# A gated mix of a long convolution and a windowed attention: GpSimd's arithmetic moved to VectorE, the large loads moved to GpSimd's queue

## The chip, the cores and the metric

The kernel runs on one core of one Trainium2 chip. The metric is the device time of one execution in microseconds (us). A core has TensorE (PE in the profile, with its weight loads as PEld), VectorE (DVE), ScalarE (ACT), GpSimd (POOL) and SyncE (SP). Each works through its own instruction stream in order. Transfers are issued by SP, ACT or POOL from that same stream and run on the core's 16 DMA engines.

## The reference

Two branches share the input `x = A_q` (2048 rows of 640) and are mixed row by row by a gate `g`. Branch A is a 4-tap convolution of `k` along the sequence, times `v`, then a long convolution with `ssm_k` (by FFT), plus `kv * ssm_D`, times `q`. Branch B is an attention of 32 heads of width 20, in which each query sees 8 keys, two rows apart.

```python
g = sigmoid((x * gate_w).sum(-1, keepdims=True))
# branch A
k_shift = sum over t of k_pad[:, t:t+S, :] * shift_k[:, 3-t]
kv = k_shift * v
y = irfft(rfft(kv padded to 2S) * rfft(ssm_k padded to 2S))[:S] + kv * ssm_D
a = q * y
# branch B
q, k, v = split(x @ wqkv)
logits = q . k[pos - 2*w] * Dh**-0.5 for w in 0..7, masked where pos - 2*w < 0
b = (softmax(logits) . v[pos - 2*w]) @ wo
return g * a + (1 - g) * b
```

## The kernel before

All work of the core is cut into small units (one PSUM slot each, four slots of two banks), and every kind of unit is a Python generator. A planner (`Plan.run`) merges the generators into one order per engine: it keeps a model of each engine's and queue's time, and at every step takes the request with the smallest start time plus 120 ns times a priority (`PRI`). It also chooses ACT or DVE for each copy out of PSUM (`AD` requests). What the planner decides is an order only. On the chip each engine runs its list in order and waits on semaphores.

The stages, with the names that the profile shows:

- **Head.** Eight loads of `x` (`xn`) are transposed (L440, 10 matmuls each) into `xT`, copied by DVE. From `xT` come 18 value projections (`psv`, L510, 10 matmuls of 320 columns each, copied to `VW`) and 30 query and key projections (`pj`, L557, 10 matmuls each, cast to `stg`). One gate projection (`gps`, L524) gives `g_nat` and `omg = 1 - g`.
- **Fragments.** `fragger` (L596) moves each finished `stg` by SBUF-to-SBUF transfers on SP into the key and query sets `kb`, `qb` (three of each), whose mask rows GpSimd has written before (L420 to L422).
- **Attention.** For each of 8 groups of 4 heads: scores `sc` (L618), exponentials on ACT (L625, 10 per group, into `ETall`), weighted sums `O` (L646), normalisation on DVE (L655, L658) into `oS`.
- **Short convolution.** `k` is loaded into `kin` (part of tile `KX`) and `v` into `vin`, eight loads each. DVE makes 4 multiplications and 3 additions for each chunk of 8 of the 64 row positions (`taps`, L454 and L461), and the product with `v` (L465). GpSimd does the same for row positions 0 to 7 (`conv_g`, buffer `pgb`).
- **Transforms.** Eight loads bring `ssm_k` to `h_lin` (in the space of `xn`), GpSimd adds `ssm_D` (L726). Then for the two halves P of the channels, and for both `h` and the convolved product `u`: first stage (L679, 10 units of 8 matmuls), second stage (L695, 11 units of 8 or 12). `h` of half 0 lands in tile `SX` (the space of `KX`, so it waits for the end of the convolution), of half 1 in `Hs`, `u` in `UC`. Swapped copies `Hw` of `h` come by transfers. Products on DVE (L779, 16 in all, 8 for each half). Inverse first stage (L791, 10 units of 16 matmuls for each half), cast into `UC`.
- **Output projection.** `oS` is transposed (L809) to `oT`, 16 units `op` (L825) are scaled by `omg` on ACT into `bl`.
- **End.** `load_q` (L841) loads `q` once more, 4 transfers, into the space of `SX`, after the inverse of half 0 has read it. `qscale` (L848) multiplies it by `g`, 16 instructions of 128x640. `final` (L869) makes the last inverse stage, six groups of three row blocks (the sixth has one): ACT casts it to `yb`, DVE multiplies by the scaled `q` (L881) and adds `bl` (L883), SP stores (L886).

In this kernel SP issues every large load, in one stream with the fragments: a request of `load` waits in the planner until the transfers before it are nearly done (`bg=1500`). ACT issues 16 transfers before its first computation (L403 to L411). GpSimd writes masks and ones, issues five small transfers, computes its share of the convolution, adds `ssm_D` and scales `q`. Each queue uses eight completion semaphores in turn, so a transfer waits for the one eight places ahead of it.

Of the kernel before, what the change touches and what calls it, by code (L numbers as in the profile page):

```python
# [13 lines left out]
ALU = mybir.AluOpType  # L14
# [32 lines left out]
CR = 8  # L47
GR = 8
# [81 lines left out]
class Req:  # L130


    def __init__(self, engs, cost=0.0, deps=(), take=0, give=(), n=0, move=0.0, pri=None, mode=None, bg=None, mm=0, lean=0.0):
        self.engs, self.cost, self.deps, self.take, self.give, self.n, self.move = engs, cost, deps, take, give, n, move
        self.pri, self.mode, self.bg, self.mm, self.lean = pri, mode, bg, mm, lean
# [4 lines left out]
LEAN_QK = 1040.0  # L140
LEAN_V = -285.0
LEAN_H = -39.0
PRI = dict(loads=0, fragger=0, xpose=1.5, score_gen=0.0, pv_gen=1.0, conv=3.0, conv_v=5.5, conv_g=0, conv_end=0, qkproj=2.1, vproj=2.7, gate=5.7,
           load_G=0, h_slot=0, u_slot=0, swaps=0, load_T=0, op_tr=-7.6, outproj=14.1, load_q=0, qscale=0, final=3.6, h_stream=(6.3, 5.2),
           u_stream=(10.8, 10.0), mults=(-3.3, 5.2), inverse1=(8.0, 7.7))
# [4 lines left out]
class Plan:  # L150


    def __init__(self, nslots):
        self.at = dict(P=0.0, A=0.0, D=0.0, G=0.0, S=0.0, Q=0.0)
        self.mode = None
        self.count = 0
        self.page = 0.0
        self.pipe = 0.0
# [13 lines left out]
    def start(self, r, e):  # L172
# [12 lines left out]
        if r.bg is not None:  # L185
            t = max(t, self.pipe - r.bg)
# [10 lines left out]
    def run(self):  # L197
        while self.streams:
# [31 lines left out]
            if r.move:  # L230
                at = max(self.pipe, st + 1300.0)
                self.pipe = at + r.move
                g.done = Ev(self.pipe + 700.0, "X")
# [15 lines left out]
def kernel(  # L249
# [96 lines left out]
    def load(name, dst, src, us, deps=(), bg=None, q="S"):  # L346
        g = yield Req(q, 500.0, deps, move=us, bg=bg, pri=None if bg is None else 1)
# [5 lines left out]

    def rows32(ap, q, n0, n1):
        return raw(ap, n0 * D + QC * q, [[64 * D, 32], [D, n1 - n0], [1, QC]])

    def loads():
# [7 lines left out]
        for a in range(4, 8):  # L365
            yield from load_x(a)
        for c in (1, 0):
            for q in range(4):
                yield from load(f"k{q}{c}", kin[32 * q:32 * q + 32, 3 + 32 * c:35 + 32 * c, :], rows32(k2, q, 32 * c, 32 * c + 32), 1400.0, (), 1500.0)
        for c in range(2):  # L370
            for q in range(4):
                yield from load(f"v{q}{c}", vin[32 * q:32 * q + 32, c], raw(v2, QC * q + 80 * c, [[64 * D, 32], [D, 64], [1, 80]]), 2050.0, (), 1500.0)
        yield Req("S", 1.0, [ev("convG")])
        h_lin = p0.tile([128, 80, 2, 64], BF, name="h_lin", tag="HL")
        st["h_lin"] = h_lin
        for c in range(2):
            for q in range(4):
                yield from load(f"h{q}{c}", h_lin[32 * q:32 * q + 32, :, c, :],
                                raw(A_ssm_k, (160 * q + 80 * c) * S, [[64, 32], [S, 80], [1, 64]]), 2200.0, (), 1500.0)

    def load_G():
        yield Req("S", 1.0, [ev("conv"), ev("grow"), ev("vproj")])
# [18 lines left out]

    def heads():
# [3 lines left out]
        for q in range(4):  # L406
            nc.scalar.dma_start(wraw[32 * q:32 * q + 32].rearrange("p c j -> p (c j)"), raw(A_shift_k, 4 * QC * q, [[0, 32], [1, 4 * QC]]))
        for q in range(4):
            for a, b in ((1, 17), (17, 32)):
                nc.scalar.dma_start(kin[32 * q + a:32 * q + b, 0:3, :], raw(k2, (64 * a - 3) * D + QC * q, [[64 * D, b - a], [D, 3], [1, QC]]))  # L410
        nc.scalar.dma_start(F[:], cf["F"].ap())  # L411
# [515 lines left out]
```

## Time and profile before

| | |
|---|---|
| median of 3 runs | 300.77 us (298.35 to 301.0) |
| the profiled execution, its own time | 300.68 us |
| its span, first to last instruction | 298.9 us |
| PE busy | 222.3 us (74%) |
| DVE busy | 208.6 us (70%) |
| ACT busy | 153.8 us (51%) |
| POOL busy | 77.9 us (26%) |
| granted TensorE clock, mean | 0.833 |

Busy shares are means over stages with different limits, so the profile is read by stage. Stretches are cut at events of PE: first score matmul at 57.3 us, end of the last query or key projection at 134.2, end of the last weighted sum at 161.5, last second-stage transform matmul at 215.7, first inverse matmul at 231.2, end of the inverse at 249.3. What ends last in each stretch sets its length.

### The profile page before, as it was taken

To read this page: it belongs to the slowest core of one execution; us is meant where nothing else is said; L and a number is where in the kernel's file an instruction comes from. 1 tells how busy PE (TensorE), PEld (TensorE's weight loads), DVE (VectorE), ACT (ScalarE), POOL (GpSimd) and SP (SyncE) were. 2 spreads that over 40 slices of the span, in tenths; PEclk is the share of its full clock that TensorE was granted. 3 is DMA by queue.
4 is the path that set the end of the run, shared out by engine and by line. 5 is a ranking of instruction groups with operands and counts; after the bars stand their busy time and mean duration, and the time that the engine had idled before them with its cause. 6 is when DMAs were issued, how large, how long until landed. Compare 5 with 4: busy or idle time off the path is not lost. (4 is left out here: it accounts for less than half of the span.)

```text
span 298.9 us, 8211 instructions
## 1 busy us (share of the span) xinstructions
PE 222.3 (74%) x3639; PEld 171.5 (57%) x3646; DVE 208.6 (70%) x214; ACT 153.8 (51%) x186; POOL 77.9 (26%) x57
## 2 busy tenths in 40 slices
PE   3789996379898999598889998975899997122000
PEld 2779784146655666366667887764577996111000
DVE  1135899999769999497888899858499343035472
ACT  0232210244454875288988699876465876023210
POOL 3996099810100000100000000000000000199990
PEclk9999997778977999796555999999599999655555
DMA  7999982918955999445800003999400009702333
GB/s 245 311 266 165 153 117 52 140 22 132 133 86 108 133 135 120 83 110 156 270 8 5 3 2 68 219 219 212 133 0 2 2 15 210 133 3 68 92 106 89
DMA packets 58587, 33.82 MB, mean 113 GB/s; under 512 B 48184, under 2 KB 55096, under 8 KB 57912
## 3 DMA queue, kind: packets, MB, share of 16 engines
q1 hardware_dynamic: 57000, 32.50, 56.5%
q10 hardware_dynamic: 1392, 0.80, 1.0%
q8 instruction: 28, 0.46, 0.7%
q14 instruction: 7, 0.06, 0.1%
q0 software_dynamic: 160, 0.00, 0.1%
HBM read 20.01 MB, written 2.62 MB: 76 GB/s over the span
## 5 line engine op out<-in xcount | busy, mean ns | idle before, releaser
L625 ACT ACTIVATE ETall<-sc 121x912 bf16<-121x912 f32 (+1 forms) x80 | 64.1, 854 | 38.2 <-PE sc L618 36.5
L848 POOL TENSOR_SCALAR SX<-SX,g_nat 128x640 bf16<-128x640 bf16 x16 | 30.8, 1939 | 138.5 <-DMA SX<-in_A_q_dram 138.5
L557 PE MATMUL pj<-xT,Wqk 128*128 128x342 bf16 (+1 forms) x300 | 56.8, 343 | 4.1 <-DVE stg L278 3.6
L557 PEld LDWEIGHTS <-Wqk 128*128 128x128 bf16 x300 | 30.0, 105 | 22.4 <-issue 4.5
L618 PE MATMUL sc<-qb,kb 31*128 31x114 bf16 x576 | 24.1, 246 | 14.1 <-DMA vin<-in_A_v_dram 4.9
L278 DVE CAST stg<-pj 128x684 bf16<-128x684 f32 (+1 forms) x30 | 26.6, 888 | 9.0 <-PE pj L557 4.5
L510 PE MATMUL psv<-KX,xT 128*121 128x320 bf16 x180 | 30.4, 323 | 2.9 <-ACT VW L276 1.9
L454 DVE TENSOR_TENSOR KX<-KX 128x1280 bf16<-128x1280 bf16 x28 | 30.9, 1116 | 2.1 <-DMA g_nat<-KX 1.8
L510 PEld LDWEIGHTS <-xT 128*121 128x121 bf16 x180 | 25.9, 148 | 5.3 <-issue 3.5
L618 PEld LDWEIGHTS <-kb 31*128 31x128 bf16 x576 | 14.6, 107 | 25.1 <-issue 19.6
L276 ACT CAST VW<-psv 121x640 bf16<-121x640 f32 x17 | 11.6, 697 | 31.1 <-PE psv L510 31.1
L881 DVE TENSOR_TENSOR SX<-yb,SX 128x1920 bf16<-128x1920 bf16 (+1 forms) x6 | 9.2, 1538 | 25.4 <-POOL SX L848 25.4
L276 ACT CAST UC<-s 128x960 bf16<-128x960 f32 (+2 forms) x25 | 22.4, 966 | 8.2 <-PE s L695 8.0
L695 PEld LDWEIGHTS <-SX 64*128 64x128 bf16 x512 | 20.0, 98 | 10.7 <-issue 9.6
L825 PE MATMUL op<-wo,oT 128*128 128x512 bf16 (+1 forms) x153 | 24.5, 312 | 0.4
L461 DVE TENSOR_TENSOR KX<-KX 128x1280 bf16<-128x1280 bf16 x21 | 23.4, 1114 | 1.3 <-DMA g_nat<-KX 0.9
L876 ACT CAST yb<-i 128x960 bf16<-128x960 f32 (+1 forms) x12 | 9.9, 873 | 25.4 <-DVE SX L881 17.8
L278 DVE CAST UC<-s 128x1024 bf16<-128x1024 f32 (+1 forms) x17 | 19.3, 1193 | 4.1 <-PE s L695 3.3
L869 PE MATMUL i<-UC,T 32*32 32x160 bf16 x512 | 6.9, 288 | 19.6 <-ACT yb L876 9.8
L825 PEld LDWEIGHTS <-oT 128*128 128x128 bf16 x160 | 16.8, 148 | 7.0 <-issue 1.5
L278 DVE COPY xT<-tx 128x1280 bf16<-128x1280 bf16 x8 | 6.5, 822 | 20.0 <-PE tx L440 20.0
L278 DVE CAST SX<-s 128x1024 bf16<-128x1024 f32 (+1 forms) x15 | 17.1, 1187 | 1.7 <-PE s L679 1.6
(65 smaller groups left out, 373.6 us busy)
## 6 DMA issues: line engine op xcount, KB each, us to landing
xn<-in_A_q_dram SPq DMA_DIRECT2D x8, 320.0 KB
KX<-in_A_k_dram SPq DMA_DIRECT2D x8, 320.0 KB
vin<-in_A_v_dram SPq DMA_DIRECT2D x8, 320.0 KB
h_lin<-in_A_ssm_k_dram SPq DMA_DIRECT2D x8, 320.0 KB
Hw<-SX SPq DMA_DIRECT2D x4, 640.0 KB
Hw<-Hs SPq DMA_DIRECT2D x4, 640.0 KB
SX<-in_A_q_dram SPq DMA_DIRECT2D x4, 640.0 KB
out_dram<-SX SPq DMA_DIRECT2D x20, 120.0 KB
```

What stands on the lines that cost most here:

```text
L276: nc.scalar.copy(dst, src)
L278: nc.vector.tensor_copy(dst, src)
L454: eng.tensor_tensor(d, kin[:, n + 3 - j:n + 3 - j + m, :], w.to_broadcast([128, m, QC]), ALU.mult)
L461: eng.tensor_tensor(ta if j else dst, ta, tb, ALU.add)
L510: nc.tensor.matmul(ps[0:BK, n0 // 320, 0:320], lhsT=xT[:, dt, s0:s0 + BK], rhs=Wv[:, dt, n0:n1], start=(dt == 0), stop=(dt == NDT - 1))
L557: nc.tensor.matmul(ps[:, i, 0:n], lhsT=Wqk[:, dt, w, 128 * ft:128 * ft + 128], rhs=xT[:, dt, s0:s0 + n], start=(dt == 0), stop=(dt == NDT ...
L618: nc.tensor.matmul(sc[:, hh, BQ * bb:BQ * bb + BQ], lhsT=kb[r:r + DH + NF, BK * b:BK * b + 128], rhs=qb[r:r + DH + NF, BQ * b:BQ * b + BQ] ...
L625: nc.scalar.activation(ETall[0:BK, e, :, 0:BQ * nb], sc[0:BK, :, 0:BQ * nb], ACT.Exp, scale=SCALE)
L695: nc.tensor.matmul(ps[:, c, 160 * jj:160 * jj + 160], lhsT=st["G"][rows, j0 + jj, rr, :], rhs=Am[rows, rr].rearrange("p o (q j) l -> p j ( ...
L825: nc.tensor.matmul(op[:, n0:n1], lhsT=oT[:, ft].rearrange("p h m a -> p a (h m)")[:, t, :], rhs=wo[:, ft, n0:n1], start=(ft == 0), stop=(f ...
L848: nc.gpsimd.tensor_scalar(qg[:, t, :], qg[:, t, :], g_nat[:, t:t + 1], None, ALU.mult)
L876: nc.scalar.copy(yb[:, 0:m, 320 * k:320 * k + 320].rearrange("p n (q c) -> p q n c", q=2), pss[k][:, :, 0:160 * m].rearrange("p q (n c) -> ...
```

## The change

GpSimd keeps its mask and constant writes and the one addition of `ssm_D`. Its share of the convolution (`conv_g`) and the scaling of `q` go to DVE. The convolution now runs over all 64 row positions in chunks of 11 (five of 11 and one of 9: 42 instructions of up to 1760 elements where there were 49 of 1280), the product with `v` in 4 pieces of 32 positions. The loads of `k`, `v`, `ssm_k`, `G`, `wo`, `T` and `q` are issued by GpSimd, in a generator `bulk` of their own, as are 13 of the 16 transfers that ACT issued (4 of `wraw`, 8 of the rows before `kin`, and `F`). `masks(2)` and the ones in `ETall` and `VW` are written between the loads of `k` and `v`. DVE clears a buffer and PE runs 8 matmuls of 512 columns on it before the first transpose. The planner's leans and priorities are other numbers, its model has a transfer pipe for each queue, and `bg` is gone.

```diff
-CR = 8
-GR = 8
+CR = 11
+WARM = 8
...
-LEAN_QK = 1040.0
-LEAN_V = -285.0
-LEAN_H = -39.0
...
+LEAN_QK = -370.0
+LEAN_V = 53.0
+LEAN_H = 195.0
...
+    def bulk():
         for c in (1, 0):
             for q in range(4):
-                yield from load(f"k{q}{c}", kin[32 * q:32 * q + 32, 3 + 32 * c:35 + 32 * c, :], rows32(k2, q, 32 * c, 32 * c + 32), 1400.0, (), 1500.0)
+                yield from load(f"k{q}{c}", kin[32 * q:32 * q + 32, 3 + 32 * c:35 + 32 * c, :],
+                                raw(k2, 32 * c * D + QC * q, [[64 * D, 32], [D, 32], [1, QC]]), 2200.0, [ev("x3")], "G")
+        g = yield Req("G", 4000.0)
+        masks(2)
...
+        nc.gpsimd.memset(ETall[:, :, :, 3 * BQ:], 1.0)
...
-        for q in range(4):
-            nc.scalar.dma_start(wraw[32 * q:32 * q + 32].rearrange("p c j -> p (c j)"), raw(A_shift_k, 4 * QC * q, [[0, 32], [1, 4 * QC]]))
...
+        z = pab[:, 0].rearrange("p n c -> p (n c)")
+        nc.vector.memset(z, 0.0)
+        wu = psp.tile([128, 2, 512], F32, name="wu", tag="ps0")
+        for n in range(WARM):
+            nc.tensor.matmul(wu[:, n % 2, :], lhsT=z[:, 0:128], rhs=z[:, 0:512], start=True, stop=True, skip_group_check=True)
...
-        for n in range(64 - CR, GR - 1, -CR):
...
+        hi = 64
+        while hi:
+            m = min(CR, hi)
+            n = hi - m
...
-    def conv_g():
...
-            for n in range(GR, 64, 28):
...
+            for n in range(0, 64, 32):
...
     def load_q():
-        yield Req("S", 1.0, [ev("i10")])
+        yield Req("G", 1.0, [ev("i10")])
...
-            nc.sync.dma_start(qg[32 * g:32 * g + 32], raw(x2, (32 * (g // 2) + g % 2) * D, [[64 * D, 32], [2 * D, 16], [1, D]]))
+            nc.gpsimd.dma_start(qg[32 * g:32 * g + 32], raw(x2, (32 * (g // 2) + g % 2) * D, [[64 * D, 32], [2 * D, 16], [1, D]]))
...
     def qscale():
         for t in range(16):
-            r = yield Req("G", 700.0, [ev("qg"), ev("gate")])
+            r = yield Req("D", 310.0, [ev("qg"), ev("gate")])
             qg = st["qg"]
-            nc.gpsimd.tensor_scalar(qg[:, t, :], qg[:, t, :], g_nat[:, t:t + 1], None, ALU.mult)
+            nc.vector.tensor_scalar(qg[:, t, :], qg[:, t, :], g_nat[:, t:t + 1], None, ALU.mult)
```

GpSimd's stream from its second mask set on, before (lines of the kernel before):

```order
L420 MEMSET kb_81 128x8
L421 COPY kb_81<-mm 128x2178
L422 COPY qb_82<-mm 128x2052
L423 MEMSET ETall 128x16x128
L424 MEMSET VW 128x576
L426 MEMSET VW 7x32 x2
L427 DMA wgz<-in_gate_w_dram 128x5x1
L429 DMA Dz<-in_A_ssm_D_dram 1x16x10 x4
L454 ISA
L454 TENSOR_TENSOR pgb<-KX 128x1280 x2
```

and in the changed kernel (its own line numbers; L346 is the helper that issues a load, `KX` holds `kin`):

```order
L440 DMA F<-cf_F 128x384
L346 DMA KX<-in_A_k_dram 32x32x160 x8
L410 MEMSET kb_81 128x8
L411 COPY kb_81<-mm 128x2178
L412 COPY qb_82<-mm 128x2052
L372 MEMSET ETall 128x16x128
L373 MEMSET VW 128x576
L375 MEMSET VW 7x32 x2
L346 DMA vin<-in_A_v_dram 32x64x80 x8
L346 DMA h_lin<-in_A_ssm_k_dram 32x80x64 x8
L728 ISA
L728 TENSOR_TENSOR h_lin<-h_lin,Dz 128x160
```

The arithmetic on `pgb` is gone, and 24 loads stand around the third mask set and the ones, with nothing of another kind between the last two blocks.

VectorE's stream at the start of the convolution, before (L278 copies out of PSUM, L454 and L461 are the convolution's multiplications and additions):

```order
L278 COPY xT<-tx 128x2x5x128 x4
L278 CAST stg<-pj 128x2x342
L278 COPY xT<-tx 128x2x5x128 x2
L469 COPY KX<-KX 128x640
L278 COPY xT<-tx 128x2x5x128
L278 CAST stg<-pj 128x2x342
L278 COPY xT<-tx 128x2x5x128
L454 TENSOR_TENSOR KX<-KX 128x1280 x2
L278 CAST stg<-pj 128x2x342
```

and in the changed kernel (L276 copies out of PSUM, L465 and L472 are the convolution; the rows left out are more of L465 and L472 alone):

```order
L419 MEMSET KX 128x880
L276 COPY xT<-tx 128x2x5x128 x8
L480 COPY KX<-KX 128x640
L465 TENSOR_TENSOR KX<-KX 128x1760 x2
L472 TENSOR_TENSOR KX<-KX 128x1760
...
L276 CAST stg<-pj 128x2x363
L465 TENSOR_TENSOR KX<-KX 128x1760
```

21 instructions of the convolution now stand before VectorE's first cast of a projection. Of the 30 such casts VectorE keeps 17 and ScalarE has 13.

VectorE's stream at the end, before (L881 and L883 are the last product and sum) and after it the changed one (L850 is the scaling of `q`, L883 and L885 the last product and sum):

```order
L278 CAST UC<-i_4005 128x128x8
L278 CAST UC<-i_4061 128x128x8
L881 TENSOR_TENSOR SX<-yb_4002,SX 128x1920
L883 TENSOR_TENSOR SX<-SX,bl 128x1920
L881 TENSOR_TENSOR SX<-yb_4002,SX 128x1920
```

```order
L276 CAST UC<-i_3949 128x128x8
L276 CAST UC<-i_4005 128x128x8
L850 TENSOR_SCALAR SX<-SX,g_nat 128x640 x16
L883 TENSOR_TENSOR SX<-yb_4040,SX 128x1920
L885 TENSOR_TENSOR SX<-SX,bl 128x1920
```

The 16 scalings stand between the last cast of the inverse and the first product. On PE the tenth and last inverse unit of half 0, which `load_q` waits for, is the 12th of the 20 inverse units with 3 `op` units among them, where it was the 15th with none.

## Rows read from the trace of the kernel before

**Rows 1.** The chain that ended last, in order of time: start us, us, what.

```profile
231.37 13.41 PE i L791 x240
...
246.19 14.27 DMA SX<-in_A_q_dram
...
272.90 16.75 POOL SX L848 x9
...
289.67 1.76 DVE SX L881
...
293.03 0.02 issue
293.05 0.49 DVE SX L883
```

**Rows 2.** Groups of instructions: busy us and mean ns, idle before, releaser.

```profile
L848 POOL TENSOR_SCALAR SX<-SX,g_nat 128x640 bf16<-128x640 bf16 x16 | 30.8, 1939 | 138.5 <-DMA SX<-in_A_q_dram 138.5
```

**Rows 3.** By stretch: length, busy PE, PEld, DVE, ACT, POOL (instructions); clock, DMA share, GB/s.

```profile
57.30:134.20 76.90, 68.75 (x972) 44.08 (x976) 66.41 (x90) 42.57 (x53) 5.17 (x4) 0.88 0.74 107
134.20:161.50 27.30, 24.16 (x562) 18.43 (x564) 22.53 (x28) 24.25 (x31) 0.00 (x0) 0.56 0.40 124
161.50:215.70 54.20, 45.93 (x857) 38.22 (x858) 44.63 (x40) 40.97 (x47) 0.00 (x0) 0.91 0.53 118
215.70:231.20 15.50, 15.31 (x109) 11.40 (x111) 14.31 (x11) 9.69 (x13) 0.00 (x0) 1.00 0.00 1
```

**Rows 4.** Timeline of DVE: start us, us, engine, line, operation, idle before.

```profile
50.01 3.11 DVE L454 TENSOR_TENSOR KX<-KX 128x1280 bf16<-128x1280 bf16 x1
...
72.12 0.82 DVE L461 TENSOR_TENSOR KX<-KX 128x1280 bf16<-128x1280 bf16 x1
...
291.46 1.16 DVE L883 TENSOR_TENSOR SX<-SX,bl 128x1920 bf16<-128x1920 bf16 x1
```

**Rows 5.** Timeline of POOL, same columns.

```profile
7.97 2.00 POOL L421 COPY kb<-mm 128x2178 bf16<-128x2178 bf16 x1 [4.35 <-DMA mm<-ca_mm]
...
25.07 2.03 POOL L429 DMA_DIRECT2D Dz<-in_A_ssm_D_dram x4
...
49.37 3.07 POOL L461 TENSOR_TENSOR pgb<-pgb 128x1280 bf16<-128x1280 bf16 x1
...
121.25 0.94 POOL L726 TENSOR_TENSOR h_lin<-h_lin,Dz 128x160 bf16<-128x160 bf16 x1 [39.33 <-DMA qb<-stg]
```

**Rows 6.** Timeline of ACT, its first computation.

```profile
13.33 1.28 ACT L276 ACT_TABLE_LOAD   x1 [13.33 <-DMA KX<-in_A_k_dram]
```

**Rows 7.** Timeline of PE in the head.

```profile
6.36 2.89 PE L510 MATMUL psv<-KX,xT 128*121 128x320 bf16 x10 [1.01 <-DMA KX<-in_B_wqkv_dram]
...
23.18 1.52 PE L510 MATMUL psv<-KX,xT 128*121 128x320 bf16 x10
24.54 0.72 PE L440 MATMUL tx<-ident,xn 128*128 128x128 bf16 x10
25.09 1.52 PE L510 MATMUL psv<-KX,xT 128*121 128x320 bf16 x10
...
27.01 1.62 PE L557 MATMUL pj<-xT,Wqk 128*128 128x342 bf16 x10
...
57.30 0.56 PE L618 MATMUL sc<-qb,kb 31*128 31x114 bf16 x8 [4.94 <-DMA vin<-in_A_v_dram]
```

**Rows 8.** Timeline of SP's queue: start of the first issue, time over all.

```profile
15.68 14.99 SPq L348 DMA_DIRECT2D KX<-in_A_k_dram x8
...
47.69 5.30 SPq L596 DMA_DIRECT2D kb<-stg x7
```

**Rows 9.** Groups of DVE instructions, shapes kept apart.

```profile
L881 DVE TENSOR_TENSOR SX<-yb,SX 128x1920 bf16<-128x1920 bf16 x5 | 8.7, 1748 | 25.4 <-POOL SX L848 25.4
...
L469 DVE COPY KX<-KX 128x640 bf16<-128x640 bf16 x1 | 0.5, 483 | 0.0
...
L538 DVE TENSOR_SCALAR omg<-g_nat 128x16 f32<-128x16 f32 x1 | 0.2, 174 | 0.0
```

More of the change, by code (lines that the diff above doesn't have):

```diff
@@ L130, with __init__ @@
 class Req:
[L133 removed]
+    def __init__(self, engs, cost=0.0, deps=(), take=0, give=(), n=0, move=0.0, pri=None, mode=None, mm=0, lean=0.0):
         self.engs, self.cost, self.deps, self.take, self.give, self.n, self.move = engs, cost, deps, take, give, n, move
[L135 removed]
+        self.pri, self.mode, self.mm, self.lean = pri, mode, mm, lean
 LAT = {("P", "A"): 230.0, ("P", "D"): 230.0, ("A", "P"): 120.0, ("D", "P"): 120.0, ("A", "D"): 100.0, ("D", "A"): 100.0}
 SWITCH = 110.0
[L140 to L145 removed]
+LEAN_QK = -370.0
+LEAN_V = 53.0
+LEAN_H = 195.0
+PRI = dict(loads=0, fragger=0, xpose=-8.5, score_gen=-1.4, pv_gen=1.9, conv=3.5, conv_v=5.1, bulk=0, conv_end=0, qkproj=2.0, vproj=-7.0, gate=5.7,
+           load_G=0, h_slot=0, u_slot=0, swaps=0, load_T=0, op_tr=6.4, outproj=4.9, load_q=0, qscale=0, final=11.8, h_stream=(2.5, 4.7),
+           u_stream=(5.8, -3.9), mults=(-7.4, 9.9), inverse1=(2.9, 1.2))
 PAGE = 256
@@ L230, in run @@
             if r.move:
-                at = max(self.pipe, st + 1300.0)
-                self.pipe = at + r.move
-                g.done = Ev(self.pipe + 700.0, "X")
+                at = max(self.pipe[e], st + 1300.0)
+                self.pipe[e] = at + r.move
+                g.done = Ev(self.pipe[e] + 700.0, "X")
                 self.lane[e].append(g.done.t)
@@ L344, with load @@
     st = {}
-    def load(name, dst, src, us, deps=(), bg=None, q="S"):
-        g = yield Req(q, 500.0, deps, move=us, bg=bg, pri=None if bg is None else 1)
+    def load(name, dst, src, us, deps=(), q="S"):
+        g = yield Req(q, 700.0 if q != "G" else 300.0 + 0.7 * us, deps, move=us)
         dict(S=nc.sync, Q=nc.scalar, G=nc.gpsimd)[q].dma_start(dst, src)
@@ L469, in conv @@
         nc.vector.tensor_copy(wl, wraw.rearrange("p c j -> p j c"))
-        at("wl", 0.0)
-        c0 = 60.0 + 0.55 * CR * QC
-        for n in range(64 - CR, GR - 1, -CR):
-            g = yield Req("D", c0, [ev(f"k{q}{c}") for q in range(4) for c in range(2) if c or n < 35])
-            for _ in taps(nc.vector, n, CR, pab[:, 0], pab[:, 1], kin[:, n + 3:n + 3 + CR, :]):
+        hi = 64
+        while hi:
+            m = min(CR, hi)
+            n = hi - m
+            c0 = 150.0 + 0.525 * m * QC
+            g = yield Req("D", c0, [ev(f"k{q}{c}") for q in range(4) for c in range(2) if (c or n < 35) and (hi > 32 or not c)])
+            for _ in taps(nc.vector, n, m, pab[:, 0, 0:m], pab[:, 1, 0:m], kin[:, n + 3:n + 3 + m, :]):
                 g = yield Req("D", c0)
+            hi = n
         mark("convD", g)
@@ L612, in score_gen @@
                 for k in range(2):
-                    g = yield Req("P", 2 * nb * 28.0 + 30.0, [ev(f"set{t}"), ev("ET")], take=1, mode="s", mm=2 * nb)
+                    g = yield Req("P", 2 * nb * 28.0 + 30.0, [ev(f"set{t}")], take=1, mode="s", mm=2 * nb)
                     sc = psum(g, "sc")
@@ L889 @@
     heads()
-    for gen in (loads, fragger, xpose, score_gen, pv_gen, conv, conv_v, conv_g, conv_end, qkproj, vproj, gate, load_G, h_slot,
+    for gen in (loads, fragger, xpose, score_gen, pv_gen, conv, bulk, conv_v, conv_end, qkproj, vproj, gate, load_G, h_slot,
                 u_slot, swaps, load_T, op_tr, outproj, load_q, qscale, final):
```

88 lines of the change are left out of this document (40 added, 48 removed).

## The prediction, made before the changed kernel ran

> **What bounds the kernel now.** I read the chain that ended last first, then the stretches, then single timelines. The chain [rows 1] shows PE at the inverse until 231.37 + 13.41 = 244.8 us, then nothing but the reload of `q` until 246.19 + 14.27 = 260.5, then GpSimd's scaling (one piece alone is 16.75 us), then VectorE's last pair. The scaling is 16 instructions and 30.8 us [rows 2]. VectorE ends at 293.05 + 0.49 = 293.5, and the span at 298.9, so the stores cost 5.4 us more. From the end of the inverse of half 0 (call it X, 244.8) the tail is 298.9 - 244.8 = 54.1 us, in which PE has little to do.
>
> Ahead of X, PE is busy in most of every stretch [rows 3], but not at one limit: from 57.3 to 134.2 PE has 68.75 and VectorE 66.41 of 76.9 us, from 134.2 to 161.5 ScalarE has 24.25 of 27.3 (its exponentials), from 161.5 to 215.7 nobody is over 46 of 54.2 and the copies out of PSUM share the work. In the head PE waits: ScalarE computes nothing before 13.3 us, because it issues transfers [rows 6], and the first score stands behind 4.94 us of waiting for loads in SP's stream [rows 7]. Where GpSimd computes beside VectorE, VectorE's convolution instruction takes 3.11 us, and 0.82 where GpSimd is idle [rows 4, 5].
>
> **The head.** PE's work ahead of the first score is, in the changed order, 8 transposes, 18 value projections, 9 `pj` and the gate, where it was 8, 15 and 8. From start to start a warm value projection takes 24.54 - 23.18 = 1.36 us and a transpose 25.09 - 24.54 = 0.55 [rows 7]. A `pj` shows 1.62, some 0.15 of it under the next unit as with the value projection: 1.5. The gate is put at 1.2, an estimate from its 20 matmuls against a unit's 10 of about two thirds the width. The first value projection started at 6.36 and ran cold (2.89 us against 1.52). Eight matmuls of 512 columns ahead of it take about 0.4 us each cold (2.89 for 10 of 320 columns, scaled), so 3.5 us, start after a clearing of 880 elements, and end near 5.5; the value projections begin at 7 but warm. ScalarE has three transfers left instead of 16, so its copies no longer hold PE. The key set of the first group needs 18 value and 6 `pj` units: 7 + 7 x 0.55 + 18 x 1.36 + 6 x 1.5 = 44.3, its cast 0.9, and then the fragments. Lower bound: seven issues of 5.30 us [rows 8] and 2 for landing, 52.5; upper: as before, 57.3 - 47.7 = 9.6 from the first issue, 54.8. I take 52.5, as no load stands in SP's stream any more. That is 4.8 us earlier, with 3 x 1.36 + 1.5 + 1.2 = 6.8 us more of PE's work done: 11.6 us ahead.
>
> **The convolution and the loads.** GpSimd reaches the loads of `k` so: masks at 8.0 [rows 5], two sets of 3.9, four small clears and transfers (4.0), nine small transfers at 2.03 / 4 = 0.51 each (4.6): 24.5 us. What one issue of 1024 rows costs on its queue no row shows: below, 0.51; above, 14.99 / 8 = 1.87, SP's [rows 8]. I take 1.5, near the upper row, which is of the same transfer. The four loads that the first chunk needs are issued by 30.5 and landed by about 35.5. One instruction of 1760 elements is put between 0.82 for 1280 and 1.16 for 1920 [rows 4], 1.08; 21 of them stand ahead of VectorE's first cast, so that cast comes at 58 us, and PE's tenth `pj` (done near 54) waits for it, with three other slots to go on. Of VectorE's remaining work to the last cast (21 x 1.08, 4 products of about 1.45, 16 casts of 0.88, four normalisations of 2.6) there are 53 us: it could end at 111. PE needs 76.9 - 6.8 = 70.1 us from 52.5, 122.6. So PE's pace decides, and VectorE's block costs nothing unless `k` is late. If nothing of the block hides, it costs 58 - 52.5 = 5.5 us, and this stays in the upper end. GpSimd's own eight instructions like the one shown [rows 5] cost VectorE some 2.3 us each, but before 60 us, so this gain is already in the head.
>
> The 16 loads of `v` and `ssm_k` follow the masks and ones (about 9 us), from 46 us. At 1.5 to 3.0 us each (the same upper row, doubled for rows twice as many) they end between 70 and 94. They are needed near 100 and 125. Before, the last landed at 121.25 [rows 5], so there is room.
>
> **The middle.** From the last `pj` to the last weighted sum both orders hold the same 216 score and 240 sum matmuls, ScalarE bound: 27.3 us again, 122.6 + 27.3 = 149.9. From there to the last second-stage matmul (54.2 before) PE loses three `op` units of 1.41 (11 of them fill the 15.5 us [rows 3]) and 48 second-stage matmuls, done earlier, and gains 16 of the first stage: 5.3 us less, 48.9, to 198.8. VectorE's products move behind this point, but ten `op` units (14.1 us) cover the eight of half 0 (11.3). Then X lies after 12 inverse units of 13.41 / 15 = 0.894 and three `op`: 14.1 + 10.7 + 4.2 = 29.0, as before (29.1). X = 227.8.
>
> **The tail.** The reload takes 15.7 us again, and 0.5 more through GpSimd. Scaling on VectorE: no row has it. Below it, the scalar form on 16 elements, 0.174; above it, a copy of the same 640 elements at 0.483 [rows 9]; between, 0.33, so 16 x 0.33 = 5.3 us (2.8 to 7.7). Then five pairs of 1.75 and 1.16 [rows 4, 9] and one of 0.98: 15.5. The stores 5.4. The sum is 16.2 + 5.3 + 15.5 + 5.4 = 42.4 instead of 54.1. PE's last stage starts 8 inverse and two `op` units after X, 10 us, under the reload.
>
> The Trainium skill, "VectorE: DVE Perf Modes", the perf-mode tier table, gives this kind of instruction four elements a cycle in bf16. By its arithmetic the scaling would be an estimated 0.32 us each, 5.2 in all; no run here shows it yet.
>
> Sum: 227.8 + 42.4 = 270.2 us of span, against 298.9; the time lies 1.8 above the span (300.68, beside a median of 300.77): **272 us**.
>
> **The rivals.**
> *Descriptors held by VectorE.* If GpSimd can't write its transfers while VectorE reads two SBUF operands, as it can't compute beside it (3.11 against 0.82 [rows 4]), the 16 loads advance only in VectorE's gaps. Its 51 us of convolution lie in the 70 from 36 to 106, which leaves 27%: 1.5 / 0.27 = 5.6 us each, 46 + 90 = 136 for the last, needed at 125, PE's first `h` unit being stuck in order. Cost 10 to 13 us: **284**. For it, the contention in the rows; against it, that those rows are of arithmetic that reads.
> The Trainium skill, "SBUF — State Buffer", "Who interferes with whom", has a lock that blocks GpSimd's descriptors under VectorE's two-port copies and scalings, and exempts two-input operations because they take the read side only. By that rule the loads here are free, and only the 16 scalings, behind all loads, would hold anything; the 3.11 us agree with its clause on reads.
>
> *The head's gain is given back.* VectorE and PE hold 89% and 86% of the stretch from 57.3 [rows 3]; if the order's waits stretch with what starts earlier, only the tail is won: 300.7 - 11.7 = **289**. For it, that two engines are near full there; against it, that 13 casts go to ScalarE, which has 42.57 of 76.9.
>
> *Slower: GpSimd's queue can't feed the transforms.* The place is the addition of `ssm_D`, which waits for the last `ssm_k` load; PE's first `h` unit stands behind it. My gain is 28.5 us, so it is lost when `h_lin` is whole later than 125 + 28.5 = 153. From 24.5 that is 128 us for 24 loads, 5.4 each. Before, they spanned 15.68 to 121.25, 4.4 each, but with SP waiting for casts in between; `k` alone took 1.87. At 6 us each: 168, **316**. Nothing shows such a price; no row shows the queue loaded either.
>
> *More.* Granted clock was 0.88 from 57.3; without stalls, 12% of 68.75 is 8 us: **264**.
>
> **How the numbers follow.** The forecast with its bounds (scaling -2.5 to +2.4, fragments +2.3, block +5.5, middle -5 to +5) holds 264 to 280, chance 0.63. More than it, below 264, 0.10. Descriptors held or late `k`, 280 to 287, 0.11; head given back, 287 to 297, 0.08; within 1% of 300.8, 0.03; slower by over 1% (GpSimd's queue), 0.05. One per cent is about what a measurement of this kernel can tell from no change. A range of 260 to 288 leaves out some 0.04 below and 0.14 above. Faster 0.92, same 0.03, slower 0.05.
>
> **What would show it.** Right: first score near 52; VectorE's convolution near 1.08 us each throughout; last `pj` near 123; the addition of `ssm_D` before 120; X near 228; no POOL in the chain's end; scalings near 0.33. Wrong: VectorE's first convolution after 42 us, or PE idle for `h_lin`, points to the queue; a last `pj` after 130 to the head's gain given back; scalings that begin later than 17 us after X to the reload.

## The result, and the profile after

The changed kernel takes **282.56 us** (median of 4 runs, 280.38 to 282.92) against 299.86 for the kernel before: a ratio of 0.941, 95% interval 0.934 to 0.948. The forecast was 272 with a range of 260 to 288. The profiled execution took 282.82 us with a span of 281.0 at a mean granted clock of 0.837.

Parts of the page after: busy time; the span in 40 slices of 7.0 us (PE, VectorE, ScalarE, DMA in tenths); the queues (packets, MB, share of 16 engines); the chain by line.

```profile
PE 216.7 (77%) x3654; PEld 166.9 (59%) x3654; DVE 189.8 (68%) x213; ACT 161.8 (58%) x197; POOL 60.5 (22%) x79
...
PE   6999999216900898999985999888999999991320
...
DVE  2142079940502899999885878999998995411992
ACT  1333543033801387886884878999965588771460
...
DMA  6953999999995114233598100019579000495085
...
q0 software_dynamic: 4368, 14.84, 29.0%
q1 hardware_dynamic: 8072, 18.04, 26.3%
...
PE psv L512 9%; DMA kb<-stg 8%; PE op L827 7%; PE pj L559 6%; DMA g_nat<-KX 5%; DMA SX<-in_A_q_dram 5%; PE s L697 5%; DMA qb<-stg 5%; DVE UC L276 4%; PE sc L620 4%; PE i L793 4%; DVE Hs L276 3%; DVE stg L276 3%; DVE KX L465 3%; PE O L648 3%; DVE SX L885 2%
```

GpSimd's scaling, which stood in the chain before [rows 1, 2], is gone. In its place 18% of the span is DMA of things that are small: fragments of `kb` and `qb`, and `g_nat`. The slices say where: PE reads 2, 1 in the eighth and ninth and 0, 0 in the twelfth and thirteenth, while the DMA engines are at 9 without a break from the fifth to the twelfth slice.

The forecast and the trace, stage by stage (us; X is the end of the inverse of half 0, as in the prediction):

| | first score | last `pj` | last weighted sum | last second stage | X | end of span |
|---|---|---|---|---|---|---|
| forecast | 52.5 | 122.6 | 149.9 | 198.8 | 227.8 | 270.2 |
| after | 61.0 | 137.7 | 170.6 | 212.0 | 241.1 | 281.0 |
| stage after, minus forecast | +8.5 | +6.6 | +5.6 | -7.5 | +0.1 | -2.5 |

The timeline of PE after (start us, us, what, idle time before and its releaser) shows the first two differences.

```profile
36.14 10.44 PE L559 MATMUL pj<-xT,Wqk 128*128 128x342 bf16 x70
46.51 1.26 PE L526 MATMUL gps<-xT,wgz 128*32 128x512 bf16 x20
47.71 3.08 PE L559 MATMUL pj<-xT,Wqk 128*128 128x342 bf16 x20
61.00 0.25 PE L620 MATMUL sc<-qb,kb 31*128 31x114 bf16 x1 [10.22 <-DMA kb<-stg]
...
76.75 0.76 PE L648 MATMUL O<-VW,ETall 121*128 121x21 bf16 x24
92.63 2.73 PE L559 MATMUL pj<-xT,Wqk 128*128 128x342 bf16 x9 [15.12 <-DVE oS L660]
```

All that the forecast put ahead of the first score (18 value projections, 9 `pj`, the gate) is done at 47.71 + 3.08 = 50.8. Then PE stands for 10.2 us, and again for 15.1. What released it, from the chain that ended last (start us, us, what):

```profile
45.55 12.76 DMA qb<-stg
58.32 11.01 DMA kb<-stg
...
74.63 15.13 DMA g_nat<-KX
89.88 1.07 DVE KX L472
...
141.54 9.47 DMA kb<-stg
```

A fragment is at most 85 KB and `g_nat`'s four transfers are 2 KB each; they take 9 to 15 us to land. By stretch (length; busy PE, PEld, DVE, ACT, POOL; clock, DMA share, GB/s), the DMA engines are full through PE's first wait and up to the second, and behind the second PE is busy nearly all the time:

```profile
50.00:61.00 11.00, 0.78 (x6) 0.32 (x4) 9.20 (x9) 1.55 (x3) 2.40 (x3) 0.64 1.05 163
61.00:77.00 16.00, 12.39 (x170) 7.48 (x171) 4.66 (x5) 9.05 (x12) 5.93 (x5) 0.72 1.04 175
77.00:93.00 16.00, 0.88 (x23) 0.67 (x20) 3.08 (x5) 0.73 (x1) 1.28 (x1) 0.60 0.70 93
93.00:138.00 45.00, 43.95 (x735) 28.71 (x735) 43.61 (x59) 33.83 (x43) 2.18 (x4) 0.95 0.30 61
```

VectorE stands in the same place: a convolution instruction, line 472, waits 15.45 us. In the tail its 16 scalings take 4.82 us (5.3 forecast), and a product takes 1.15 where 1.75 was forecast. VectorE's timeline:

```profile
73.52 0.92 DVE L276 CAST stg<-pj 128x726 bf16<-128x726 f32 x1
89.88 1.07 DVE L472 TENSOR_TENSOR KX<-KX 128x1760 bf16<-128x1760 bf16 x1 [15.45 <-DMA g_nat<-KX]
...
258.71 4.82 DVE L850 TENSOR_SCALAR SX<-SX,g_nat 128x640 bf16<-128x640 bf16 x16 [10.97 <-DMA SX<-in_A_q_dram]
263.45 1.15 DVE L883 TENSOR_TENSOR SX<-yb,SX 128x1920 bf16<-128x1920 bf16 x1
```

SP's queue starts these issues early enough, but they stretch (start of the first, time over all):

```profile
41.50 5.46 SPq L598 DMA_DIRECT2D qb<-stg  x7
47.06 11.91 SPq L598 DMA_DIRECT2D kb<-stg  x7
...
68.57 6.56 SPq L535 DMA_DIRECT2D g_nat<-KX  x4
...
76.07 15.29 SPq L598 DMA_DIRECT2D kb<-stg  x7
```

The seven issues of `kb` took 5.30 us before [rows 8] and take 11.91 and 15.29 now, because SP waits for earlier transfers of its own: over the whole run nine times for `qb`, 8.7 us, and twice for `g_nat`, 10.1. So a late landing is paid in the queue as well; in the chain above a landing of `qb` and one of `kb` stand one behind the other. Meanwhile GpSimd's loads of `v` are issued from 39.77 at 1.05 us each, those of `ssm_k` from 48.83 to 73.41 at 1.19 each, and the page has their median time from issue to landing: 13.6 and 17.2 us.

**Theory A**: the loads no longer stand in SP's queue, but they stand on the same 16 DMA engines, up to eight at a time, and SP's fragments and `g_nat` come through late among them. **Rivals**: the wait for `g_nat` alone is the loss (B); it is the number of small rows, not the bytes, that is in the way (A1 against A2); SP's issues or the new order set it (C). And in the tail: that the scaling is not what gave the 18 us.

### The profile page after: what moved, and what is told of

It is laid out like the page before. It is cut to its first block, busy times and chain, and to the rows that moved or that the text cites. A ratio compares the mean times of both kernels' runs of the same rounds, so it can differ in the third digit from the quotient of the medians.

```text
span 281.0 us, 8233 instructions
## 1 busy us (share of the span) xinstructions
PE 216.7 (77%) x3654; PEld 166.9 (59%) x3654; DVE 189.8 (68%) x213; ACT 161.8 (58%) x197; POOL 60.5 (22%) x79
## 2 busy tenths in 40 slices
DMA packets 13034, 33.81 MB, mean 120 GB/s; under 512 B 2764, under 2 KB 6872, under 8 KB 12360
## 4 chain that ended last, share of the span: by engine, by line
PE 43%; DVE 26%; DMA 23%; SPq 3%; issue 2%; POOL 1%; ACT 1%; DVEq 0%
PE psv L512 9%; DMA kb<-stg 8%; PE op L827 7%; PE pj L559 6%; DMA g_nat<-KX 5%; DMA SX<-in_A_q_dram 5%; PE s L697 5%; DMA qb<-stg 5%; DVE UC L276 4%; PE sc L620 4%; PE i L793 4%; DVE Hs L276 3%; DVE stg L276 3%; DVE KX L465 3%; PE O L648 3%; DVE SX L885 2%
## 5 line engine op out<-in xcount | busy, mean ns | idle before, releaser
L559 PE MATMUL pj<-xT,Wqk 128*128 128x342 bf16 (+1 forms) x300 | 51.6, 326 | 15.5 <-DVE oS L660 15.1
L559 PEld LDWEIGHTS <-Wqk 128*128 128x128 bf16 x300 | 28.8, 101 | 32.6 <-issue 16.4
L465 DVE TENSOR_TENSOR KX<-KX 128x1760 bf16<-128x1760 bf16 (+1 forms) x24 | 24.8, 1042 | 11.6 <-DMA KX<-in_A_k_dram 11.2
L274 ACT CAST stg<-pj 128x684 bf16<-128x684 f32 (+1 forms) x13 | 9.5, 744 | 36.9 <-DMA kb<-stg 27.6
L472 DVE TENSOR_TENSOR KX<-KX 128x1760 bf16<-128x1760 bf16 (+1 forms) x18 | 18.8, 1044 | 15.9 <-DMA g_nat<-KX 15.4
L512 PE MATMUL psv<-KX,xT 128*121 128x320 bf16 x180 | 25.7, 299 | 1.4 <-DVE xT L276 1.4
L274 ACT CAST UC<-s 128x1024 bf16<-128x1024 f32 (+1 forms) x24 | 22.6, 1000 | 4.0 <-PE s L697 3.0
L276 DVE CAST stg<-pj 128x726 bf16<-128x726 f32 (+1 forms) x17 | 15.2, 894 | 11.1 <-DMA g_nat<-KX 10.3
L276 DVE CAST UC<-s 128x960 bf16<-128x960 f32 (+2 forms) x18 | 19.9, 1139 | 1.1 <-PE s L697 1.0
L276 DVE CAST SX<-s 128x1024 bf16<-128x1024 f32 (+1 forms) x16 | 18.8, 1195 | 2.5 <-PE s L697 1.9
L827 PEld LDWEIGHTS <-oT 128*128 128x128 bf16 x160 | 16.5, 147 | 5.7
L793 PE MATMUL i<-F,Hw 128*128 128x128 bf16 x160 | 18.3, 219 | 0.0
L831 ACT ACTIVATE bl<-op,omg 128x640 bf16<-128x640 f32 x16 | 12.7, 795 | 9.2 <-PE op L827 9.2
L793 PEld LDWEIGHTS <-Hw 128*128 128x128 bf16 x160 | 17.9, 113 | 0.0
## 6 DMA issues: line engine op xcount, KB each, us to landing
vin<-in_A_v_dram POOLq DMA_DIRECT2D x8, 320.0 KB, 13.6
h_lin<-in_A_ssm_k_dram POOLq DMA_DIRECT2D x8, 320.0 KB, 17.2
SX<-in_A_q_dram POOLq DMA_DIRECT2D x4, 640.0 KB, 10.2
```

The costliest lines, as they stand in the source:

```text
L274: nc.scalar.copy(dst, src)
L276: nc.vector.tensor_copy(dst, src)
L465: eng.tensor_tensor(d, kin[:, n + 3 - j:n + 3 - j + m, :], w.to_broadcast([128, m, QC]), ALU.mult)
L472: eng.tensor_tensor(ta if j else dst, ta, tb, ALU.add)
L512: nc.tensor.matmul(ps[0:BK, n0 // 320, 0:320], lhsT=xT[:, dt, s0:s0 + BK], rhs=Wv[:, dt, n0:n1], start=(dt == 0), stop=(dt == NDT - 1))
L559: nc.tensor.matmul(ps[:, i, 0:n], lhsT=Wqk[:, dt, w, 128 * ft:128 * ft + 128], rhs=xT[:, dt, s0:s0 + n], start=(dt == 0), stop=(dt == NDT ...
```

## The experiments

Times are medians; ratios are to the kernel before as it ran beside each, with 95% intervals, and are not quotients of the medians shown. From each trace, which is of one execution (of e13 the fastest, 294.8; of e5 the slowest, 285.6): the start of the first score and of the last instruction of three groups, the last issue of `q`'s reload, and the end of the span.

| kernel | us | ratio | first score | last `pj` | last sum | last 2nd stage | reload issued | end |
|---|---|---|---|---|---|---|---|---|
| before | 299.9 | 1 | 57.3 | 133.9 | 161.4 | 215.5 | 246.2 | 298.9 |
| after | 282.6 | 0.941 (0.934-0.948) | 61.0 | 137.4 | 170.4 | 211.8 | 243.7 | 281.0 |
| e4: before, scaling on VectorE | 283.5 | 0.943 (0.935-0.951) | 56.9 | 131.7 | 159.0 | 212.8 | 243.5 | 280.2 |
| e13: after, scaling on GpSimd | 298.3 | 0.994 (0.987-1.002) | 60.8 | 136.2 | 168.2 | 209.7 | 241.6 | 293.0 |
| e5: after, no warming | 282.8 | 0.938 (0.933-0.942) | 62.3 | 137.5 | 170.3 | 215.2 | 247.0 | 283.7 |
| e1: after, own `grow` | 278.2 | 0.926 (0.918-0.933) | 61.3 | 132.5 | 165.8 | 207.2 | 239.1 | 276.5 |
| e3: after, long rows | 273.6 | 0.911 (0.903-0.918) | 65.6 | 129.3 | 161.2 | 202.7 | 234.5 | 271.7 |
| e8: after, 4 in flight | 276.9 | 0.920 (0.916-0.924) | 60.5 | 132.0 | 163.7 | 205.1 | 237.0 | 274.2 |
| e2: after, 2 in flight | 267.9 | 0.888 (0.878-0.897) | 54.3 | 123.6 | 156.1 | 197.1 | 229.0 | 266.4 |
| e10: e2, no warming | 269.3 | 0.899 (0.895-0.904) | 55.5 | 122.2 | 154.3 | 198.6 | 230.5 | 267.6 |
| e6: e2 and e1 | 265.0 | 0.881 (0.876-0.885) | 53.5 | 118.0 | 151.4 | 192.7 | 224.6 | 262.0 |
| e7: e6, `G`, `wo`, `T` held | 259.6 | 0.861 (0.856-0.866) | 53.2 | 116.1 | 145.2 | 186.4 | 218.2 | 255.7 |
| e14: e7, old order | 269.8 | 0.902 (0.897-0.907) | 52.4 | 128.1 | 151.1 | 202.5 | 231.0 | 267.9 |
| e12: e7, reload in parts | 255.4 | 0.854 (0.848-0.859) | 53.3 | 120.4 | 149.5 | 190.9 | 222.2 | 254.8 |

**e4, the scaling alone on VectorE, in the kernel before.**

```
-            nc.gpsimd.tensor_scalar(qg[:, t, :], ...
+            nc.vector.tensor_scalar(qg[:, t, :], ...
```

> The kernel before, with q's scaling on VectorE and nothing else changed. Theory: the tail shortens by the scalings' time on GpSimd and by the longer pairs beside them, 10 to 14 us, so 286 to 290 us; that is most of the 18 us that the whole change gave. Rival (the tail's gain comes from the queue, the clock or the earlier reload): 295 to 300 us.

Measured 283.5: one word of the diff gives 16.5 us, nearly as much as the whole change (17.3), and more than the 10 to 14 that I had expected. From the reload's landing to VectorE's last sum it takes 16.6 us (258.0 to 274.6), where it took 33.0 [rows 1]. Its timeline of VectorE, with products of 1.15 instead of 1.75 [rows 9]:

```profile
258.04 1.27 DVE L848 TENSOR_SCALAR SX<-SX,g_nat 128x640 bf16<-128x640 bf16 x4 [10.23 <-DMA SX<-in_A_q_dram]
259.23 1.15 DVE L881 TENSOR_TENSOR SX<-yb,SX 128x1920 bf16<-128x1920 bf16 x1
```

**e13, the reverse: the changed kernel without that word.**

```
-            nc.vector.tensor_scalar(qg[:, t, :], ...
+            nc.gpsimd.tensor_scalar(qg[:, t, :], ...
```

> Changed kernel with q's scaling back on GpSimd, the order of the rest unchanged. Theory (the scaling carries nearly all of the change's gain, since the rest gives back between 61 and 93 us what it wins): 296 to 300 us, within 1.5% of the kernel before. Rival (the parts overlap, and the rest has a gain of its own): 288 to 293 us.

Measured 298.3, which can't be told from the kernel before. The two runs together split the change: the scaling is worth 16, and the queue, the convolution on VectorE, the warming and the new order together some 1 us by the medians, with up to 4 inside e13's interval. GpSimd's row (POOL) and VectorE's in this run, from two timelines:

```profile
255.89 29.79 POOL L850 TENSOR_SCALAR SX<-SX,g_nat 128x640 bf16<-128x640 bf16 x16 [13.67 <-DMA SX<-in_A_q_dram]
```

```profile
267.12 1.75 DVE L883 TENSOR_TENSOR SX<-yb,SX 128x1920 bf16<-128x1920 bf16 x1 [1.97 <-POOL SX L850]
268.90 1.82 DVE L885 TENSOR_TENSOR SX<-SX,bl 128x1920 bf16<-128x1920 bf16 x1
```

A scaling takes GpSimd 1.86 us and VectorE 0.30, and beside GpSimd's scaling VectorE's sum grows from 1.16 to 1.82.

**e5, without the warming matmuls.** `WARM = 0`.

> Changed kernel without the eight warming matmuls; the rest of the order is unchanged. Theory (in the changed kernel the first scores wait for late fragments, so what the head gains is eaten there): projections of v run at the lower clock at first and end 3 to 5 us later, but the time moves by less than 2 us, 281 to 285 us. Rival (the head's gain stands): 285 to 289 us.

Measured 282.8: nothing moved. PE's head is later, and the wait for fragments takes up half of that (timeline of PE):

```profile
50.32 3.08 PE L559 MATMUL pj<-xT,Wqk 128*128 128x342 bf16 x20
62.34 0.25 PE L620 MATMUL sc<-qb,kb 31*128 31x114 bf16 x1 [8.95 <-DMA kb<-stg]
```

The last two projections start at 50.32 instead of 47.71, so PE is 2.6 us behind; it waits 1.3 us less, the first score is 1.3 later, and by the last `pj` (137.5 against 137.4) nothing is left of it.

**e1, the gate's exponentials out of KX.** `grow` is a view of KX, the tile in which the convolution runs. Its columns are not the convolution's, but the first convolution instruction behind the `g_nat` transfers waits for them all the same.

```
-    grow = KX[:, 0:1024].bitcast(F32)
+    grow = p0.tile([128, 512], BF, name="grow")     # and g_nat's source in bf16
```

> Changed kernel, but the gate's exponentials get a tile of their own (bf16, 1 KB a partition) instead of a view of KX; the order on every engine is unchanged. Theory A (the four 2 KB transfers into g_nat land 15 us late among GpSimd's loads, and the convolution waits for them only because they read KX): the 15.4 us wait of line 472 is gone, VectorE goes on at 74.5, and since the next fragments of kb are late for the same reason, only part of it is kept: 270 to 277 us. Rival B (the kb fragments behind it are as late and hold the same work): 281 to 283 us, the idle time moves to the scores or to the copies into stg.

Measured 278.2, between the two. The wait of line 472 is gone, but only 4.9 of its 15.4 us reach the last `pj`, since the next fragments are as late. In the kernel before the same dependency cost little; the waits for `g_nat` (us in total, times, longest) before, and after:

```profile
DVE KX L454 <- DMA g_nat<-KX: 1.8, 1, 1.8
DVE KX L461 <- DMA g_nat<-KX: 0.9, 1, 0.9
```

```profile
DVE KX L472 <- DMA g_nat<-KX: 15.4, 1, 15.4
```

The chain of e1:

```profile
53.78 12.17 DMA kb<-stg
...
77.88 10.99 DMA kb<-stg
```

**e2, at most two loads in flight.** Before each load of `v` and `ssm_k` GpSimd copies one element of what the load two places earlier brought, and so waits for it.

```
+    def paced(q, one):
+        if len(sent) >= 2:
+            a, ap = sent[-2]
+            nc.gpsimd.tensor_copy(pace[32 * a:32 * a + 1, 0:1], ap)
+        sent.append((q, one))
...
+                paced(q, vin[32 * q:32 * q + 1, c, 0, 0:1])
                 yield from load(f"v{q}{c}", ...
```

> Changed kernel, with a one-element copy on GpSimd ahead of each load of v and of the convolution kernel that reads what the load two places earlier brought, so that at most two of these loads are in flight instead of eight; the order of everything else is unchanged. Theory A (fragments and g_nat stand among the rows of up to eight loads): a fragment lands in 3 to 5 us, first score at 52 to 56 instead of 61, the waits of 15 us at 74 to 92 shrink to under 6, last projection at 122 to 128, time 266 to 274 us. Rival C (SP's own issue and its order of fragments set it): first score still at 60 to 61, time 280 to 284. Rival D (the loads become late by the pacing): addition of ssm_D after 120, time above 284.

Measured 267.9, 14.7 us under the changed kernel, by a delay. First score at 54.3, last `pj` starting at 123.6: near the 52.5 and 122.6 of the prediction. SP's order of issues is the same, so C falls: the seven issues of `kb` take 5.18 us again, where they took 11.91, so SP's stretched issues were a consequence. Rival D falls too: the addition of `ssm_D` moves from 90.5 to 103.6 and nobody waits for it. SP's queue in e2, then what is left in its chain:

```profile
47.61 5.18 SPq L609 DMA_DIRECT2D kb<-stg  x7
```

```profile
49.89 7.68 DMA kb<-stg
...
66.33 4.26 DMA g_nat<-KX
...
127.19 9.43 DMA kb<-stg
```

**e8, four in flight.** As e2 with `sent[-4]`.

> As e2_paced with four loads in flight instead of two. Theory A (a fragment waits behind what is in flight, so its delay grows with the depth): first score between 55 and 61, time between the two, 271 to 278 us. Rival (the tiny copies on GpSimd help by something else than depth, such as by keeping GpSimd from writing descriptors): the same as with two, 266 to 270 us.

Measured 276.9, between the two as A says, so the depth matters and not the one-element copies as such; but not in proportion: first score 60.5, as late as with eight (61.0), and the gain comes later. The loads land in 11.2 and 10.9 us (`v`, `ssm_k`), against 13.6 and 17.2 with eight and 6.8 and 7.0 with two.

**e3, the same bytes in long rows.** For instance

```
-  raw(v2, QC * q + 80 * c, [[64 * D, 32], [D, 64], [1, 80]])
+  raw(v2, 0, [[64 * D, 32], [1, 64 * 80]])
```

> Changed kernel, with the loads of k, v and the convolution kernel reading the same number of bytes into the same tiles as rows of 10 KB instead of 320, 160 and 128 bytes; they fetch other elements, so the convolution's data are not the reference's. Theory A1 (the number of small rows in flight is what fragments wait behind): GpSimd's loads land in about 3 us each, first score at 51 to 54, no wait above 5 us between 60 and 95, time 264 to 272. Rival A2 (the bytes in flight are what matters, whatever the rows): first score at 58 to 61, time 278 to 283.

Measured 273.6; neither expectation held. The first fragments are later still, 65.6, so A1 falls for the head: it is not the number of small rows. The kernel is 9 us faster all the same. The loads are through sooner (the addition of `ssm_D` at 70.6 instead of 90.5), the wait for `g_nat` is 1.9 us, and the later fragments land in 3.84; that the first is the cause of the others is argued, as the loads of `v` also fetch the same bytes eight times here (chain):

```profile
43.51 13.36 DMA qb<-stg
56.88 13.84 DMA kb<-stg
...
85.46 3.84 DMA kb<-stg
```

**e6, both: paced, and `grow` in its own tile.**

> Changed kernel with both: at most two loads of v and of the convolution kernel in flight, and the gate's exponentials in a tile of their own. With pacing alone the convolution still waited 4.3 us for g_nat on the chain. If that wait is a loss of its own: 262 to 265 us, last projection some 3 to 4 us sooner than with pacing alone (125). If the fragments behind it take its place: 266 to 269 us.

Measured 265.0, 2.9 us under e2 with intervals that overlap; the last `pj` is 5.6 sooner, and e2's wait of 4.6 us for `g_nat` is gone. With the fragments on time that wait is a loss of its own, which e1 alone could hardly show.

**e7, `G`, `wo` and `T` behind the last fragment.**

```
         at("SX", 0.0)
+        yield Req("G", 1.0, [ev("frags")])
+        nc.gpsimd.tensor_copy(pace[96:97, 0:1], ksets[1][96:97, 0:1])
         for a in range(4):       # loads of G
```

> As e6_both, and the loads of G, wo and T wait, by a one-element copy on GpSimd, until the last fragment of kb has landed. Theory A (what fragments share the DMA engines with sets when they land, here too): the wait for kb between the last projection and the last weighted sum (9.4 us on the chain of the paced kernel) falls to 3 or less, that stage is 27 to 29 us instead of 32.5, time 3 to 5 us under e6_both, 259 to 263 us. Rival (that stage is long for ScalarE's exponentials or the order, and G is then late for the second transform stage): no gain or a loss, 265 to 272 us.

Measured 259.6. The stage from the last `pj` to the last sum is 29.1 us, where it was 33.4 in e6 and 33.0 after, and 27.3 was forecast, and no transfer of `kb` stands in its chain there any more: the third late stage had the same cause. e7's stretch from 118 to 147, about that stage (length; busy PE, PEld, DVE, ACT, POOL; clock, DMA share, GB/s):

```profile
118.00:147.00 29.00, 27.50 (x582) 21.11 (x580) 24.69 (x32) 24.27 (x31) 3.80 (x7) 0.59 0.50 163
```

**e10, e2 without warming.**

> As e2_paced (267.9), without the warming matmuls. In the unpaced kernel their removal moved nothing. Theory (what they gain is eaten by late fragments, and stands where fragments are on time): 2 to 5 us slower than e2_paced, 270 to 273 us. Rival (they gain nothing anywhere): 267 to 269 us.

Measured 269.3, 1.4 us over e2, between the two expectations, with intervals that overlap. First score 1.2 us later, last `pj` 1.4 sooner. What the warming is worth stays open; by these medians it is a us or two, inside the noise.

**e14, e7 planned with the old priorities.** `PRI` and the three leans as in the kernel before.

> As e7_hold_G (259.6), planned with the priorities and leans of the kernel before. The stage from the last weighted sum to the last second-stage matmul took 41 us in the changed kernel where 49 was forecast and 54 stood before. If the new order is what shortened it: that stage is 46 to 54 us and the time 264 to 275 us. If it is the loads that no longer run in it, or GpSimd's absence: 41 to 43 us, and 258 to 263 us.

Measured 269.8. The stage that came out shorter than forecast, from the last sum to the last second stage, is 51.4 us with the old numbers and 41.2 with the new. So the order shortened it, and not the loads or GpSimd. The old order is shorter from the last `pj` to the last sum (23.0 against 29.1) and longer ahead of it (75.7 against 62.9 from the first score): it puts the same work elsewhere, and 10 us are lost in all.

**e12, e7 with the reload in parts.** Three parts along t, and each group's scalings ahead of its pair.

```
+        for t0, t1 in ((0, 3), (3, 9), (9, 16)):
+            for g in range(4):
+                nc.gpsimd.dma_start(qg[32 * g:32 * g + 32, t0:t1], ...
...
+            for t in range(t0, t0 + m):         # in final, ahead of the product
+                nc.vector.tensor_scalar(qg[:, t, :], qg[:, t, :], g_nat[:, t:t + 1], None, ALU.mult)
```

> As e7_hold_G (259.6), with the reload of q cut along t into three parts of four transfers, and each group's three scalings put right ahead of its pair of products. Theory (in the tail the reload, the sixteen scalings and the pairs stand one behind the other): the first pair starts when the first yb is there, some 8 to 10 us sooner than with one reload, the last part of the reload then sets the end of it, 252 to 256 us. Rival (the final matmuls, their copies on ScalarE or the stores set the tail as soon as VectorE waits less): 257 to 260 us.

Measured 255.4, 4.2 us under e7. From the last issue of the reload to the end it takes 32.6 us instead of 37.5. The parts also start sooner: their first issues stand at 207.3, 213.6 and 220.4, two of them ahead of X (220.1 here), as each part overwrites only a piece of `SX`. VectorE's timeline: the first scalings no longer wait for a transfer, and the first pair waits for ScalarE's copy.

```profile
226.69 0.97 DVE L893 TENSOR_SCALAR SX<-SX,g_nat 128x640 bf16<-128x640 bf16 x3
232.94 1.16 DVE L895 TENSOR_TENSOR SX<-yb,SX 128x1920 bf16<-128x1920 bf16 x1 [5.27 <-ACT yb L887]
```

So in the tail what the scaling had stood behind was the whole reload. This version beats both kernels: 0.854 of the kernel before.

## Why the prediction was right, and where it was not

The time fell into the range, and the sign was right, but the gain was 17 to 18 us, not 28.5, and nearly all of it came from one part. That it fell inside is in part luck: three stages came out 20.7 us too long, and one stage and the tail 10.0 too short; without these 10 the time would have been near 293, outside the range. My own upper bounds (2.4, 2.3, 5.5 and 5) add up to 15, and the 280 of the likeliest band took in half of that. By the steps:

- **Head, PE's own work: right.** Value projections warm from 7.2 us, 18 of them, nine `pj` and the gate done at 50.8.
- **Head, the fragments: the step that failed.** "Lower bound: seven issues of 5.30 us [rows 8] and 2 for landing, 52.5 ... I take 52.5, as no load stands in SP's stream any more." The loads were out of the queue, and still the first score came at 61.0, outside my bounds. In the prediction's terms, the issues of `kb` start at 47.06 instead of 45.2 and take 11.91 instead of 5.30; from their end to the first score it is 2.0, as put. They take so long because SP waits for fragments that land 11 to 13 us after their issue. I counted the queue and left out the engines that it shares; the 2 us of landing had no row. e2 shows it: the same queue, fewer loads in flight, issues of 5.18 us and a first score at 54.3.
  The Trainium skill, "DMA: Bandwidth & Descriptors", "Issuing engines are not separate DMA queues", says that transfers of all engines run on the same 16 DMA engines and that issuing from several saves only the time to issue. This case agrees: SP's stream is clear of the loads, and its fragments land later all the same. I had not weighed that rule, and it spoke against the part of the change that moves the loads.
- **PE's pace to the last `pj`, 70.1 us: wrong by 6.6,** for the same reason, with a wait that I had not seen at all: VectorE's convolution, whose block I had put at no cost, stands behind `g_nat`. The waits cost clock as well: the first projections behind them took 3.10 and 3.01 us instead of 1.6. Without the late transfers and with `grow` in its own tile 122.6 was cautious: e6 has 118.0, e7 116.1.
- **VectorE's block and GpSimd's issues: right in kind.** First convolution at 36.56 (35.5), 1.07 us each (1.08). An issue costs 0.78 for `k`, 1.05 for `v`, 1.19 for `ssm_k`; I took 1.5 for `k`, between bounds that hold, and 1.5 to 3.0 for the other two, which is too much.
- **Last `pj` to last sum, 27.3: 5.6 short.** "Again" was true of ScalarE's work, but `G`, `wo` and `T` now run into the last fragments. Without that, e7 has 29.1; 1.8 us are left without a cause shown.
- **Last sum to last second stage, 48.9: 7.5 too long.** I counted what the order moved out of the stage, and not that it is packed better; e14 has 51.4 with the old numbers. The cause is the order; which of its moves, I did not take apart.
- **Last second stage to X, 29.0: right,** 29.1.
- **Tail, 42.4: right in kind,** 39.9. Scalings 4.8 (5.3), stores 5.2 (5.4), reload with its issue 17.6 (16.2). The pairs were mis-sized: 12.3, not 15.5, because I took 1.75 for the product from rows in which GpSimd scaled beside it. So the move of the scaling was worth more than I had put it.
  The Trainium skill, "VectorE: DVE Perf Modes", the perf-mode tier table, had led to an estimate of 0.32 us a scaling; the trace agrees, with 4.82 / 16 = 0.30.

Two of the signs that I had named for being wrong came: a last `pj` after 130, and scalings later than 17 us behind X (17.6). Of the rivals, *descriptors held by VectorE* did not happen: GpSimd's queue issued all through the convolution, at 1.05 to 1.19 us. *Slower* did not either, as `h_lin` was whole at 90. *More* did not: the granted clock from the first score to the last `pj` fell to 0.83, with the waits, where it was 0.88; in e7, without most of them, it is 0.92. *The head's gain is given back* (289) is near to what happened: the tail won 14.2 of the 17.9 us between the two spans, and e13 leaves some 1 us for the rest. But the mechanism was another than the one that I gave: VectorE and PE were not full, they stood still together from 77.5 to 89.9. I gave it 0.08, and no rival named the DMA engines.

Left open: whether a fragment waits behind rows already queued on a DMA engine or takes turns with them. That with four in flight the first score is as late as with eight, and with long rows later, speaks against a simple queue in proportion to the loads in flight; no run here shows a single DMA engine. No run undoes the move of the loads alone either, so what it is worth by itself, in the new order, is not shown.

## What to carry to other kernels

Moving loads to another engine's queue frees the issuing engine, not the DMA engines: before such a move, list the small transfers that someone waits for while the loads run, and keep the loads few in flight there (a one-element read of an earlier load is enough, and was worth 15 us). When a change has several parts, undo the part with the clearest price by itself: here one word carried nearly all of it, and the rest had room for 23 us more (e7) once the late transfers and the wait on a shared tile were out of the way. Work that stands behind a whole transfer (the scaling behind the reload) is better cut with the transfer: 4 us here.

## What the runs showed of the hardware

- Small transfers beside eight outstanding loads: 85 KB and even 2 KB took 9 to 15 us to land, with the DMA share near 1 (the page's slices); with two loads outstanding 4 to 8.
- The same 33.8 MB are 13034 packets after and 58587 before, where SP issued the large loads. That alone did not make fragments land sooner.
- VectorE is slower beside GpSimd: while GpSimd scales (1.86 us each), a product of 1920 elements takes 1.75 instead of 1.15 and a sum up to 1.82 instead of 1.16.
- In e7's stretch from 118 to 147 the granted clock was 0.59, nearer to the lower of its two levels (1.2 and 2.4 GHz), though PE was busy for 27.5 of 29 us, and the matmuls there are the small ones of scores and sums; in the same stage of before it was 0.56 [rows 3]. So removing PE's waits did not bring the clock back.
